# One score tile of the next attention step placed ahead of the first token product, at the ends of the second and third step

## The chip, the cores and the metric

One core of one Trainium2 chip runs the whole program. The metric is the device time of one execution in microseconds (us). Traces are of one execution each.

## The reference, cut to what matters

```python
def _attn_ref(q, k, v):                      # q, k, v: (8, 12, 448, 64)
    scores = scale * np.matmul(q, k.transpose(0, 1, 3, 2))
    attn = np.maximum(scores, 0.0) ** 2 / S
    return np.matmul(attn, v)

def _moe_ref(x, w_tok1, w_tok2, w_ch1, w_ch2):   # x: attention as (8, 448, 768)
    xt = x.transpose(0, 2, 1)
    h = np.maximum(xt @ w_tok1, 0.0) @ w_tok2    # token mixing
    u = x + h.transpose(0, 2, 1)
    h2 = np.maximum(u @ w_ch1, 0.0) @ w_ch2      # channel mixing
    return u + h2
```

## The kernel before

Attention runs in 24 steps of four heads, numbered from 0; (i,c) is score tile c (0 to 6) of step i. The program order is set by hand, and each engine works through its own list in that order. One tile is four TensorE matmuls into one of two score buffers in PSUM (the on-chip memory that matmuls write to), a relu (negative values set to zero) on ScalarE into SBUF (the on-chip memory for operands), and later a squaring on VectorE:

```python
ps_att = ctx.enter_context(tc.tile_pool(name="ps_att", bufs=2, ...))   # two score buffers
ps_acc = ctx.enter_context(tc.tile_pool(name="ps_acc", bufs=1, ...))   # acc0, acc1
ps_mm  = ctx.enter_context(tc.tile_pool(name="ps_mm", bufs=2, ...))    # "bank": shared ring of two
...
def scores(i, c, alone=False):
    ps = ps_att.tile([128, 2, 512], FP32, tag="att", name="sc_ps")
    ...                                   # 4 matmuls from qkT[i]
        nc.scalar.activation(at, ps[:, :, :S], AF.Relu)
    squares.append(at)

def square(keep=0):
    while len(squares) > keep:
        at = squares.pop(0)
        nc.vector.tensor_tensor(out=at, in0=at, in1=at, op=ALU.mult)
```

`values` multiplies squared tiles by v into acc0 and acc1; `values_out` evicts them; `x_back` transposes the result (through acc0 here) and has it copied to SBUF as x; `token1` is the first token product from x, with a relu on ScalarE; `token2` is the second. `transposes(i)` makes the transposed queries and keys of step i in the two `ps_mm` banks, and VectorE copies them out to `qkT[i]`. Steps 0 to 2 and the start of step 3 are this code (cut):

```python
for i in range(DB):                       # DB = 3
    for c in range(QC):                   # QC = 7
        scores(i, c, alone=(i, c) == (0, 2))
        ...
        square(keep=1)
        if c < 3 and i > 0:
            values(i - 1, ((2, 3), (4, 5), (6,))[c])
            if c == 2:
                values_out(i - 1, split=True)
        if c in (1, 2) and i > 1:
            token2(i - 2, early=True, rs=(c - 1,))
        ...
        if c == 4 and i > 0:
            x_back(i - 1, place="acc0", copy=nc.scalar.copy if i > 1 else None)
        if (i, c) in ((1, 3), (2, 5)):
            transposes(i + 1, "bank")
        if c == 6:
            values(i, (0, 1))
            if i > 0:
                token1(i - 1)
...
i = DB
values(i - 1, (2, 3, 4, 5))
square()
values(i - 1, (6,))
values_out(i - 1, split=True)
scores(i, 0)
token2(i - 2, early=True, between=lambda: x_back(DB - 1, place="acc0"))
scores(i, 1)
token1(i - 1)
square(keep=1)
scores(i, 2)
first = channel1_begin()
```

## Time and profile before

The median is 376.17 us in four runs (375.63 to 376.41); the profiled span is 374.7 us. The first part of the page gives, for each engine, busy time, its share of the span, and the number of instructions:

```profile
PE 365.0 (97%) x4377; PEld 201.2 (54%) x4377; DVE 212.1 (57%) x414; ACT 211.0 (56%) x313; POOL 99.1 (26%) x185
```

PE is TensorE's matmuls, PEld its weight loads, which overlap them; DVE is VectorE, ACT ScalarE. An average over the span says little on a change at 20 and 28 us, so the argument rests on rows in order of time, which the prediction shows.

### The profile page before, as it was taken

The numbers are of one execution on the slowest core, as the hardware profiler recorded it, in microseconds if no ns is written. First come the engines' busy times: TensorE is split into PE (matmuls) and PEld (weight loads), VectorE is DVE, ScalarE is ACT, GpSimd is POOL, SyncE is SP. The second block draws the span as 40 slices with busy tenths as digits, with TensorE's granted clock in tenths as the row PEclk, the third lists the DMA queues.
The fourth block names the chain that finished last, engine by engine and source line by source line (L and its number), as shares of the span: only waits on it lengthen the run. The fifth ranks groups of instructions, "written<-read, shape, count | busy, mean of one in ns | idle before, by whom it ended". The sixth has DMA issues, their size and how long they took to land.

```text
span 374.7 us, 10236 instructions
## 1 busy us (share of the span) xinstructions
PE 365.0 (97%) x4377; PEld 201.2 (54%) x4377; DVE 212.1 (57%) x414; ACT 211.0 (56%) x313; POOL 99.1 (26%) x185
## 2 busy tenths in 40 slices
PE   7889999999999999999999999999999999999996
PEld 3544555455555655565455655555555654555554
DVE  2986688756576666475554684575555755131022
ACT  3987888776345468725775457752775456311400
POOL 8956348304212403430330304412210000000000
PEclk9999999999999999999999999999999999999999
DMA  8999999923998886756765877758560534233024
GB/s 150 118 197 163 179 206 172 180 39 67 128 174 171 159 146 95 115 104 154 97 101 90 117 141 132 108 80 158 107 99 13 93 87 98 58 69 87 0 54 116
DMA packets 69566, 43.32 MB, mean 116 GB/s; under 512 B 43473, under 2 KB 66065, under 8 KB 69521
## 3 DMA queue, kind: packets, MB, share of 16 engines
q0 software_dynamic: 24496, 21.49, 40.8%
q1 hardware_dynamic: 44640, 20.75, 26.6%
q8 instruction: 34, 0.56, 0.6%
q10 hardware_dynamic: 384, 0.43, 0.4%
q14 instruction: 12, 0.09, 0.1%
HBM read 43.42 MB, written 11.01 MB: 145 GB/s over the span
## 4 chain that ended last, share of the span: by engine, by line
PE 89%; DVE 6%; ACT 1%; DMA 1%; issue 1%; POOL 0%; ACTq 0%; POOLq 0%; DVEq 0%
PE m_ps L443 29%; PE m_ps L404 28%; PE acc_ps L223 9%; PE sc_ps L190 9%; PE h_ps L353 4%; PE t_ps L312 3%; DVE at L211 2%; PE qkT_ps L140 2%; PE t_ps L294 1%; DMA q_raw<-in_q_dram 1%; DVE uT_sb L363 1%; PE t_ps L328 1%; ACT at L204 1%; DVE qkT L154 1%; PE x_ps L276 1%
## 5 line engine op out<-in xcount | busy, mean ns | idle before, releaser
L204 ACT ACTIVATE at<-sc_ps 128x896 bf16<-128x896 f32 x167 | 144.8, 924 | 49.7 <-PE sc_ps L190 49.7
L211 DVE TENSOR_TENSOR at<-at 128x896 bf16<-128x896 bf16 x168 | 97.7, 619 | 55.9 <-ACT at L204 55.9
L404 PE MATMUL m_ps<-uT_sb,wc 128*128 128x448 bf16 x564 | 115.5, 353 | 0.2 <-DVE uT_sb L363 0.2
L443 PE MATMUL m_ps<-wc,r_sb 128*128 128x384 bf16 x660 | 113.2, 326 | 0.0
L443 PEld LDWEIGHTS <-r_sb 128*128 128x128 bf16 x660 | 62.7, 98 | 46.7 <-issue 6.1
L411 ACT ACTIVATE r_sb<-m_ps 128x448 bf16<-128x448 f32 x94 | 51.3, 546 | 56.0 <-PE m_ps L404 55.6
L404 PEld LDWEIGHTS <-wc 128*128 128x128 bf16 x564 | 52.3, 98 | 53.4 <-issue 8.3
L450 DVE TENSOR_TENSOR out_sb<-m_ps,u_sb 128x384 f32<-128x384 f32 x55 | 30.5, 554 | 48.1 <-PE m_ps L443 48.1
L190 PE MATMUL sc_ps<-qkT 64*64 64x448 bf16 x672 | 53.2, 358 | 1.1 <-ACT at L204 0.9
L223 PE MATMUL acc_ps<-at,v_raw 64*64 64x448 bf16 x672 | 40.7, 351 | 1.5 <-DVE x_sb L285 0.7
L241 DVE TENSOR_SCALAR xT<-acc_ps 128x448 bf16<-128x448 f32 x45 | 26.1, 620 | 27.6 <-PE acc_ps L223 27.6
L659 POOL COPY gate<-x_sb 1x1 bf16<-1x1 bf16 x12 | 3.1, 254 | 126.9 <-DMA x_sb<-xT 126.9
L83 POOL DMA_DIRECT2D q_raw<-in_q_dram x48 | 28.9, 614 | 19.9 <-DMA wc<-in_moe_w_ch_dram 17.4
L363 DVE TENSOR_TENSOR uT_sb<-h_ps,xT 128x448 bf16<-128x448 f32 x48 | 27.7, 616 | 9.4 <-PE h_ps L353 9.3
L83 POOL DMA_DIRECT2D v_raw<-in_v_dram x48 | 29.6, 643 | 8.1 <-DMA wc<-in_moe_w_ch_dram 4.7
L338 ACT ACTIVATE r_sb<-t_ps 128x256 bf16<-128x256 f32 x36 | 11.8, 381 | 32.7 <-PE t_ps L328 28.5
L223 PEld LDWEIGHTS <-v_raw 64*64 64x64 bf16 x672 | 21.4, 106 | 15.7 <-issue 5.7
L190 PEld LDWEIGHTS <-qkT 64*64 64x64 bf16 x672 | 17.6, 105 | 21.9 <-issue 19.0
L83 POOL DMA_DIRECT2D k_raw<-in_k_dram x46 | 28.2, 634 | 1.7 <-issue 1.7
L154 DVE COPY qkT<-qkT_ps 128x896 bf16<-128x896 bf16 x44 | 25.3, 616 | 5.4 <-PE qkT_ps L140 5.4
L353 PE MATMUL h_ps<-wt,r_sb 128*128 128x448 bf16 x96 | 22.3, 353 | 0.0
L312 PE MATMUL t_ps<-x_sb,wt 128*128 128x256 bf16 x108 | 14.7, 273 | 0.0
(58 smaller groups left out, 150.7 us busy)
## 6 DMA issues: line engine op xcount, KB each, us to landing
out_dram<-out_sb SPq DMA_DIRECT2D x54, 192.0 KB, 2.9
q_raw<-in_q_dram POOLq DMA_DIRECT2D x48, 112.0 KB, 3.9
v_raw<-in_v_dram POOLq DMA_DIRECT2D x48, 112.0 KB, 4.8
k_raw<-in_k_dram POOLq DMA_DIRECT2D x46, 112.0 KB, 4.4
wc<-in_moe_w_ch_dram POOLq DMA_DIRECT2D x4, 1152.0 KB, 12.2
u_sb<-uT_sb SPq DMA_TRANSPOSE x48, 2.6
x_sb<-xT SPq DMA_TRANSPOSE x16, 3.2
k_first<-in_k_dram SPq DMA_DIRECT2D x1, 224.0 KB, 3.5
```

The costliest lines, as they stand in the source:

```text
L83: eng.dma_start(out=dst[64 * r : 64 * (r + 1)].rearrange("p g c d -> p g (c d)"), in_=src[b, h0 : h0 + 2].rearrange("g (p c) d -> p g (c d ...
L154: (nc.scalar.copy if split and r == 0 else nc.vector.tensor_copy)(sb[:, r].rearrange("n w t -> n (w t)"), parts[r][:, : 2 * S])
L190: nc.tensor.matmul(ps[64 * r : 64 * (r + 1), g, :S], lhsT=sb[h, r, 1, c * 64 : (c + 1) * 64], rhs=sb[h, r, 0, :], start=True, stop=True, s ...
L204: nc.scalar.activation(at, ps[:, :, :S], AF.Relu)
L211: nc.vector.tensor_tensor(out=at, in0=at, in1=at, op=ALU.mult)
L223: nc.tensor.matmul(ps[r][64 * g : 64 * (g + 1), :S], lhsT=v_raw[h, g, c, :], rhs=at[h, g, :], start=(c == 0), stop=(c == QC - 1), skip_gro ...
L353: nc.tensor.matmul(parts[r][:, :S], lhsT=r1[:, j, r * 128 : (r + 1) * 128], rhs=wt2[:, j, :], start=(j == 0), stop=(j == JC - 1),)
L363: nc.vector.tensor_tensor(out=uT_tiles[b // 2][:, 2 * d + r, off : off + S].rearrange("n (c p) -> n c p", c=QC), in0=parts[r][:, :S].rearr ...
L404: nc.tensor.matmul(ps[:, :S], lhsT=wc1[:, g, e * 128 : (e + 1) * 128], rhs=uT[:, g, off : off + S], start=(g == 0), stop=(g == CC - 1),)
L411: nc.scalar.activation(r2[:, e, off : off + S], ps[:, :S], AF.Relu)
L443: nc.tensor.matmul(ps[:, :HN], lhsT=r2[:, e, t * 128 : (t + 1) * 128], rhs=wc2[:, e, cols], start=(e == 0), stop=(e == EC - 1),)
L450: nc.vector.tensor_tensor(out=o[:, cols].rearrange("n (g d) -> n g d", d=128), in0=ps[:, :HN].rearrange("n (g d) -> n g d", d=128), in1=u_ ...
```

## The change

Intent: tile (2,0) at the end of the second step, and (3,0) at the end of the third, are to give ScalarE and VectorE something to do while TensorE is on the first token product.

```diff
-            scores(i, c, alone=(i, c) == (0, 2))
+            if c or i < 2:
+                scores(i, c, alone=(i, c) == (0, 2))
...
             if c == 6:
                 values(i, (0, 1))
                 if i > 0:
+                    scores(i + 1, 0)
+                    square(keep=1)
                     token1(i - 1)
...
     values_out(i - 1, split=True)
-    scores(i, 0)
     token2(i - 2, early=True, between=lambda: x_back(DB - 1, place="acc0"))
```

## The prediction

> Names used here: the program runs attention in steps of four heads; (i,c) is score tile c of step i, with i and c counted from 0, so the "second and third step" are i = 1 and 2. One score tile is four TensorE matmuls, a ScalarE relu out of PSUM, and a VectorE squaring.
>
> **What bounds the kernel now.** I read the page's chain first, then TensorE's waits from 41.9 us to the end, then the busy time by stretch.
>
> ```profile
> PE 89%; DVE 6%; ACT 1%; DMA 1%; issue 1%; POOL 0%; ACTq 0%; POOLq 0%; DVEq 0%
> ```
>
> ```profile
> PE m_ps L404 <- DVE uT_sb L363: 0.2, 1, 0.2
> PE acc_ps L223 <- DVE uT_sb L363: 0.2, 1, 0.2
> ```
>
> TensorE carries 89% of the chain that ended last. After 41.9 us it waits for other engines twice, 0.4 us together, and none of that is for a load from memory. So whatever TensorE gains or loses before 41.9 us should move the end by the same amount. The change lies in two places before that, near 20 us (end of step 1) and near 28 us (end of step 2). Next I read the time-ordered view of all engines there; columns are start, duration, engine, line, operation, count, and in brackets the idle time before it.
>
> ```profile
> 16.74 3.42 ACT L204 ACTIVATE at<-sc_ps 128x896 bf16<-128x896 f32 x4
> 19.70 0.57 PE L223 MATMUL acc_ps<-at,v_raw 64*64 64x448 bf16 x8 [0.72 <-DVE x_sb L285]
> 20.20 1.05 PE L294 MATMUL t_ps<-x_sb,wt 128*128 128x256 bf16 x8
> 21.18 0.38 PE L190 MATMUL sc_ps<-qkT 64*64 64x448 bf16 x4
> 21.29 0.60 ACT L302 ACTIVATE r_sb<-t_ps 128x512 bf16<-128x512 f32 x1 [1.12 <-PE t_ps L294]
> 21.39 0.55 PE L223 MATMUL acc_ps<-at,v_raw 64*64 64x448 bf16 x8
> 21.77 0.36 PE L190 MATMUL sc_ps<-qkT 64*64 64x448 bf16 x4
> 21.78 2.53 ACT L204 ACTIVATE at<-sc_ps 128x896 bf16<-128x896 f32 x3
> 22.72 0.62 DVE L211 TENSOR_TENSOR at<-at 128x896 bf16<-128x896 bf16 x1 [1.48 <-ACT at L204]
> 22.92 0.11 PEld L190 LDWEIGHTS <-qkT 64*64 64x64 bf16 x4 [0.37 <-issue]
> ```
>
> Here the change aims: during the first token product (20.20) ScalarE stands idle for 1.12 us and VectorE for 1.48, because no score tile is ready. TensorE itself runs without a break from 19.70 to 22.92.
>
> ```profile
> 26.19 1.08 ACT L285 COPY x_sb<-x_ps 128x1024 bf16<-128x1024 bf16 x1
> 27.00 1.15 DVE L154 COPY qkT<-qkT_ps 128x896 bf16<-128x896 bf16 x2
> 27.08 1.82 ACT L204 ACTIVATE at<-sc_ps 128x896 bf16<-128x896 f32 x2
> 27.32 0.57 PE L223 MATMUL acc_ps<-at,v_raw 64*64 64x448 bf16 x8 [0.52 <-ACT x_sb L285]
> 27.83 1.05 PE L294 MATMUL t_ps<-x_sb,wt 128*128 128x256 bf16 x8
> 28.81 1.19 PE L223 MATMUL acc_ps<-at,v_raw 64*64 64x448 bf16 x20
> 29.80 0.38 PE L190 MATMUL sc_ps<-qkT 64*64 64x448 bf16 x4
> 30.12 0.93 PE L353 MATMUL h_ps<-wt,r_sb 128*128 128x448 bf16 x4
> 31.54 0.69 DVE L285 COPY x_sb<-x_ps 128x1024 bf16<-128x1024 bf16 x1 [0.20 <-PE x_ps L276]
> 32.28 1.03 PE L294 MATMUL t_ps<-x_sb,wt 128*128 128x256 bf16 x8 [0.47 <-DVE x_sb L285]
> ```
>
> At the second place things differ. Tile (3,0) needs the transposed queries and keys of step 3, which VectorE copies out only from 27.00 to 28.15; and one of the two PSUM buffers for scores, the one of (2,5), is read by ScalarE until about 28.0 (first half of the 27.08 row). In the old order that tile ran at 29.80, when both were long done.
>
> **What the Trainium skill says.** "PSUM — Partial Sum Buffer", section "Engine vs sequencer instructions": ScalarE and VectorE queues are strict FIFO, and "MATMULs start and complete in program order". So a score tile put ahead of the token product holds that product up while it waits; nothing slips past. The trace agrees in the case at hand: during the wait of 0.72 us before 19.70 no later matmul appears. "Perfetto Trace Analysis", section "Optimization Strategy": find the gaps of the engine to be optimized, within its own regime, and make what they wait for start sooner. The gaps of 1.12 and 1.48 us are not TensorE's. Same page, section "Summary: the profiler window per engine type": the end of a TensorE instruction is estimated. I therefore count TensorE from start to start, and take an end only as a release of the next engine (the profile has 0.02 to 0.04 us between the two).
>
> **The change part by part.** No work is added or removed; each engine runs the same count of instructions. TensorE's order changes at two places, ScalarE's with it, VectorE's only at the second. Start-to-start costs, from the rows: value products of two tiles 0.38 us if 64-wide work follows (21.39 to 21.77) and 0.50 if 128-wide follows (19.70 to 20.20); a score tile 0.21 or 0.32 (29.80 to 30.12); token product 0.98 (20.20 to 21.18). ScalarE relu 0.855 (3.42 over 4) with 0.92 to its end; VectorE 0.535 each.
>
> First place. New order: values 19.70, (2,0) at 20.08, token product at 20.40, next values at 20.40 + 0.98 = 21.38 against 21.39. TensorE gains nothing. ScalarE: (2,0) is ready at 20.08 + 0.38, so its relu runs 20.48 to 21.40 instead of 21.78 to 22.70; the token relu then 21.47 (0.18 later, harmless: token2 needs it only at 22.44); relu of (2,1) at about 22.14 instead of 22.6. But (2,2) comes from TensorE at 22.92 whatever ScalarE does, and is ready at 23.30; its relu starts at 23.32, against 23.37 before (third of the 21.78 row). So of a lead of 0.4 us, 0.05 is left: ScalarE's idle time has only moved. From there to 27.3 ScalarE is full (relus, eviction, copy of x), and that is what TensorE's 0.52 us wait hangs on: value products at 27.26 instead of 27.32. VectorE runs ahead by about 0.25 us until it meets the relu of (2,4), which ends at about 26.32; then its copies of queries and keys start at 26.87 instead of 27.00 and end at 28.02.
>
> Second place. New order: values 27.26, done with at 27.64; (3,0) now waits for the buffer of (2,5) (relu 27.03 to 27.95) and for the second copy (28.02), so it finishes its start at about 28.06, a new wait of some 0.4 us. Token product about 28.3 instead of 27.83; values 28.3 + 0.98 = 29.28; token2 follows them directly: 29.28 + 0.99 + 0.12 (switch to 128-wide) = 30.39 against 30.12. That is 0.27 late. The removed score tile (0.32) repaid only part of 0.47 + 0.12. Next: eviction of the last values at 29.28 + 1.19 + 0.03 = 30.50 to 31.12, back transposes when token2 is through, 30.39 + 0.77 = 31.16; copy of x on VectorE at 31.81 to 32.50; token product at 32.54 against 32.28. The 0.47 us wait for that copy stays, since the back transposes move by as much. From here all is in the old order, TensorE full: the end moves by +0.26. With a full 0.32 between (3,0) and the token product it would be +0.33. I take +0.3.
>
> Sum: 0.0 at the first place, -0.05 carried to 27.26, +0.35 at the second: 376.11 + 0.3 = 376.4.
>
> **Rivals.** (a) The intent works: the relu of (2,0) fills the 1.12 us gap, ScalarE leads by a relu (0.855), and TensorE's waits of 0.26 (25.01, for an eviction) and 0.52 us (27.32) go. For it: both waits end on ScalarE or VectorE work. Against it: the 22.92 row, where TensorE's own order ends the lead. It would make at most 376.11 - 0.8 = 375.3. (b) The new wait is worse: the copies are still at 27.00, or TensorE pays the full switch and the token relu, now behind the relu of (3,0) on ScalarE (28.74 to 29.65, then 0.6), comes at 30.2, just ahead of the 30.39 at which token2 needs it. If it were late, another 0.3: 376.7 to 376.9. (c) The second place costs nothing, because the waits on 32.28 (0.47 us) swallow the delay: that holds only if the back transposes, which start it, do not move; they do, with token2. It would make 376.1.
>
> **Range and chances.** The three runs before spread over 0.78 us (375.63 to 376.41), more than the effect. Adding the rivals gives 375.7 to 377.0. Two per cent is 7.5 us, far above the sum of TensorE's idle time at both places, so within 2% is all but certain.
>
> **What would show it.** Right: ScalarE's idle 1.12 us before the token relu split into two shorter ones, about 0.3 before (2,0) and some before (2,2); the 0.52 us wait before the values near 27.3 still there; a new TensorE wait near 27.6 to 28.1 ended by the VectorE copy L154 or by a ScalarE relu; the token product of step 2 (32.28 before) about 0.3 us later; everything after that shifted by the same. Wrong: relu of (2,2) well before 23.3; no new wait near 27.9; that token product at or before 32.28.

## The result, and the profile after

The changed kernel took 376.48 us in the median of four runs (376.23 to 377.13) against 376.17 us; ratio 1.0013, interval 0.9995 to 1.003. A second set of rounds (told below) gave 1.0012, interval 1.0000 to 1.0024.

The chain that ended last, by engine, after:

```profile
PE 90%; DVE 3%; DMA 2%; POOL 2%; ACT 1%; issue 1%; POOLq 0%; ACTq 0%; DVEq 0%
```

TensorE still sets the end. Now the first place, rows in order of time (start, duration, engine, line, operation, count; in brackets the idle time before and what ended it):

```profile
19.57 0.57 PE L223 MATMUL acc_ps<-at,v_raw 64*64 64x448 bf16 x8 [0.75 <-DVE x_sb L285]
19.94 0.39 PE L190 MATMUL sc_ps<-qkT 64*64 64x448 bf16 x4
20.26 1.05 PE L294 MATMUL t_ps<-x_sb,wt 128*128 128x256 bf16 x8
20.38 0.92 ACT L204 ACTIVATE at<-sc_ps 128x896 bf16<-128x896 f32 x1 [0.35 <-PE sc_ps L190]
21.34 0.60 ACT L302 ACTIVATE r_sb<-t_ps 128x512 bf16<-128x512 f32 x1
22.79 0.38 PE L190 MATMUL sc_ps<-qkT 64*64 64x448 bf16 x4
23.23 0.92 ACT L204 ACTIVATE at<-sc_ps 128x896 bf16<-128x896 f32 x1 [0.26 <-PE sc_ps L190]
```

This trace reaches the first row 0.13 us sooner than the one before (19.57 against 19.70), because an input landed sooner (near 6.9 us the trace before waits 0.64 us for queries of step 0, this one doesn't), so compare distances from that row. ScalarE's gap of 1.12 us is gone: the relu of (2,0) runs in it. But (2,2), the 22.79 row, comes 3.22 us after the first row, as before (22.92 - 19.70), and ScalarE now waits 0.26 us for it.

The second place:

```profile
26.78 1.15 DVE L154 COPY qkT<-qkT_ps 128x896 bf16<-128x896 bf16 x2
26.95 2.59 ACT L204 ACTIVATE at<-sc_ps 128x896 bf16<-128x896 f32 x3
27.16 0.57 PE L223 MATMUL acc_ps<-at,v_raw 64*64 64x448 bf16 x8 [0.52 <-ACT x_sb L285]
27.98 0.38 PE L190 MATMUL sc_ps<-qkT 64*64 64x448 bf16 x4 [0.25 <-ACT at L204]
28.29 1.05 PE L294 MATMUL t_ps<-x_sb,wt 128*128 128x256 bf16 x8
29.27 1.14 PE L223 MATMUL acc_ps<-at,v_raw 64*64 64x448 bf16 x20
30.34 0.93 PE L353 MATMUL h_ps<-wt,r_sb 128*128 128x448 bf16 x4
32.53 1.03 PE L294 MATMUL t_ps<-x_sb,wt 128*128 128x256 bf16 x8 [0.47 <-DVE x_sb L285]
```

The 0.52 us wait that the intent would have removed stands. A new one has come before (3,0): the bracket says 0.25 us, and counted from start to start it is more, 27.98 - 27.16 - 0.38 = 0.44 us. From the first row to the last (the token product of step 2) it was 32.28 - 19.70 = 12.58 us; it is 32.53 - 19.57 = 12.96 us, so 0.38 us is lost.

Yet both profiled spans are 374.7 us. Of the 0.38 us, 0.13 is the earlier start of this trace. The rest lies near 182 us: a row of weight loads in the trace of before,

```profile
181.97 0.55 PEld L312 LDWEIGHTS <-wt 128*128 128x128 bf16 x6 [0.48 <-DMA x_sb<-xT]
```

waits for a transpose by DMA, and none does in the trace after. From the back transposes near 44.7 us to the last group of matmuls, TensorE took 324.18 us before (44.67 to 368.85) and 323.95 us after (44.92 to 368.87). In the traces of the experiments this stretch takes 323.96 us where it meets no such wait, and 324.00 to 324.60 us where it meets one to three. Such waits come and go between executions, so one span cannot decide a question of 0.3 us.

### The profile page after: what moved, and what is told of

Its sections match the earlier page's. It is cut to its first block, busy times and chain, and to the rows that moved or that the text cites. A ratio compares the mean times of both kernels' runs of the same rounds, so it can differ in the third digit from the quotient of the medians.

```text
span 374.7 us, 10236 instructions
## 1 busy us (share of the span) xinstructions
PE 365.7 (98%) x4377; PEld 202.0 (54%) x4377; DVE 212.5 (57%) x414; ACT 211.4 (56%) x313; POOL 99.0 (26%) x185
## 4 chain that ended last, share of the span: by engine, by line
PE 90%; DVE 3%; DMA 2%; POOL 2%; ACT 1%; issue 1%; POOLq 0%; ACTq 0%; DVEq 0%
PE m_ps L443 29%; PE m_ps L404 28%; PE acc_ps L223 9%; PE sc_ps L190 9%; PE h_ps L353 4%; PE t_ps L312 3%; PE qkT_ps L140 3%; DMA q_raw<-in_q_dram 1%; PE t_ps L294 1%; PE t_ps L328 1%; DMA k_raw<-in_k_dram 1%; ACT at L204 1%; DVE uT_sb L363 1%; POOL q_raw L83 1%; DVE at L211 1%
## 5 line engine op out<-in xcount | busy, mean ns | idle before, releaser
L338 ACT ACTIVATE r_sb<-t_ps 128x256 bf16<-128x256 f32 x36 | 11.9, 381 | 32.4 <-PE t_ps L328 28.3
```

## The experiments

For each kernel the table has the start of three TensorE groups, counted from the start of the value products near 19.7 us: the value products and the token product at the second place, and the token product of step 2. Ratios are against the kernel before of the same rounds.

| kernel | values | token product | token product of step 2 | median us | ratio (interval) |
|---|---|---|---|---|---|
| before | 7.62 | 8.13 | 12.58 | 376.17 | |
| changed | 7.59 | 8.72 | 12.96 | 376.48 | 1.0013 (0.9995 to 1.003) |
| changed again | 7.58 | 8.72 | 12.96 | 376.68 | 1.0012 (1.0000 to 1.0024) |
| first place alone | 7.59 | 8.09 | 12.54 | 376.04 | 0.9996 (0.9983 to 1.0008) |
| second place alone | 7.63 | 8.82 | 13.06 | 376.73 | 1.0016 (1.0004 to 1.0029) |
| copies early | 7.58 | 8.72 | 12.96 | 376.57 | 1.001 (0.9995 to 1.0024) |
| (3,0) behind | 7.59 | 8.09 | 13.23 | 376.94 | 0.9998 (0.9976 to 1.0019) |
| (3,0) behind, squaring held | 7.59 | 8.10 | 12.52 | 376.06 | 1.0002 (0.999 to 1.0013) |
| (2,2) supplied | 7.33 | 7.93 | 12.31 | 375.86 | 0.9986 (0.9958 to 1.0014) |

The runs of "(3,0) behind", "(2,2) supplied" and the first of "tiles in the gaps" shared rounds in which the kernel before had two of eleven runs at a mean clock of 0.994 and 0.995, 378.59 and 378.16 us; the other nine were at 0.998 or more, 375.92 to 376.86 us, mean 376.56. These two widen those intervals and lower those ratios.

**The first place alone.** Edit against the changed kernel: the move only where i == 1, and `scores(i, 0)` put back in the start of step 3.

> Only the first place is changed (tile (2,0) ahead of the first token product), the second is as before. My theory: ScalarE's lead is lost again at tile (2,2), which TensorE delivers when it did before, so the value products near 27.3 us start 0.05 us earlier against the start of the value products near 19.7 us, and the end moves by -0.05 us, ratio 1.000. Rival (the intent works): the two TensorE waits of 0.26 and 0.52 us go, up to -0.8 us, ratio 0.998.

12.54 against 12.58: 0.04 us gained, as expected. The 0.52 us wait is there, and the 0.26 us wait for an eviction is gone without effect: the next tile (2,5) waits for ScalarE's relu of (2,3) instead:

```profile
25.05 0.38 PE L190 MATMUL sc_ps<-qkT 64*64 64x448 bf16 x4 [0.17 <-ACT at L204]
```

The intent brought next to nothing here.

**The second place alone.** Edit: the move only where i == 2.

> Only the second place is changed (tile (3,0) ahead of the token product of step 1), the first is as before. My theory: tile (3,0) waits for its PSUM buffer and for the second copy of queries and keys, now ending at 28.15 us, so it pays slightly more than in the full change: token product of step 2 about 0.4 us later against the value products near 19.7 us, end +0.4 us, ratio 1.001. Rival (the waits after it swallow the delay): end unchanged, ratio 1.000.

0.48 us later, 0.08 more than expected, and slower by 0.6 us in time, by the medians of these rounds (376.73 against 376.12 us) and by the ratio. All of the change's loss is here. With the changed kernel's first place in front, ScalarE and VectorE come a little earlier and 0.10 us of it is spared.

**The copies earlier.** Edit against the changed kernel: `((1, 3), (2, 5))` becomes `((1, 3), (2, 4))` for the transposes.

> The changed kernel with the transposes of step 3 one score tile earlier, so that the copies of queries and keys are done near 27.5 us. If the wait of (3,0) is held by its PSUM buffer as well (the relu of (2,5) ends near 27.95), it starts no earlier: 8.3 to 8.4 us after the value products near 19.7 (8.41 in the changed kernel), ratio 1.001. If the copies alone hold it, it starts at 8.0 and the end is 0.35 us earlier, ratio 1.000.

VectorE's copies of queries and keys are through at 27.32 us (26.17 + 1.15), well ahead. The tile starts when it did, 8.41 us after the first row in both kernels:

```profile
28.05 0.38 PE L190 MATMUL sc_ps<-qkT 64*64 64x448 bf16 x4 [0.25 <-ACT at L204]
```

So taking away one of the two waits gives nothing: the score buffer, freed by ScalarE's relu of (2,5), holds the tile by itself. In "second place alone" the bracket names the copies. The two waits end almost together: taken singly, that relu and the second copy both end at 27.92 us in the changed kernel, and at 28.17 and 28.22 in "second place alone".

**Tile (3,0) behind the token product.** Edit against the changed kernel:

```diff
-                if i > 0:
+                if i == 1:
                     scores(i + 1, 0)
                     square(keep=1)
+                if i > 0:
                     token1(i - 1)
+                if i == 2:
+                    scores(i + 1, 0)
+                    square(keep=1)
```

> The changed kernel, but at the second place tile (3,0) stands directly behind the token product instead of ahead of it (still ahead of the last value products of step 2, so still earlier than before). By then (28.8 us) its buffer and its copies are ready. My theory: the new wait is gone and so is the loss; the end is that of the kernel before, -0.05 to 0 us, ratio 1.000. Rival (any move of that tile ahead of the value products costs, by the eviction they start): +0.2 to +0.3 us, ratio 1.001.

A miss. The wait ahead of the token product is gone (8.09), but the token product of step 2 is at 13.23, later than in the changed kernel. The ratio of 0.9998 hides this: without the two slow-clock runs of the kernel before, the means are 376.94 and 376.56 us, 0.4 us slower. Rows in order of time:

```profile
30.46 0.62 DVE L211 TENSOR_TENSOR at<-at 128x896 bf16<-128x896 bf16 x1 [0.79 <-ACT at L204]
31.01 0.62 DVE L241 TENSOR_SCALAR xT<-acc_ps 128x448 bf16<-128x448 f32 x1
31.68 0.62 PE L276 MATMUL x_ps<-ident,xT 128*128 128x128 bf16 x8 [0.57 <-DVE xT L241]
```

The squaring of (3,0) stands ahead of the eviction in VectorE's list, and its input came late, since the relu of (3,0) now lies behind the token relu. The eviction, ready since the value products, queues behind it, and the back transposes wait for that.

**The same with that squaring held back.** Edit: besides, `square()` becomes `square(keep=1)` between the last value products of step 2.

> Tile (3,0) directly behind the token product, as in the first try of that place, but its squaring is now left behind the last evictions of step 2 on VectorE instead of ahead of them. If the 0.57 us wait of the back transposes in the first try came from that squaring in VectorE's queue, it goes, and the token product of step 2 starts 12.5 to 12.6 us after the value products near 19.7 (12.58 before, 12.96 in the changed kernel, 13.23 in the first try): end -0.05 to 0 us against before, ratio 1.000. Rival (the place itself costs): still 12.9 or later, ratio 1.001 to 1.002.

12.52: the loss is gone. The tile may stand elsewhere at this place without cost if it meets its buffer free, and if its follow-up on VectorE doesn't block an eviction.

**The transposes late, in both kernels.** Edit: `((1, 3), (2, 5))` becomes `((1, 3), (2, 6))`, first in the changed kernel, then in the kernel before.

> The changed kernel with the transposes of step 3 issued one score tile later, so that their copies come on VectorE after the squaring of (2,5), near 28.5 to 29.6 us: the suspected wait of (3,0) is made about 1.6 us longer. My theory: everything behind it moves with it, 1.6 us more than the changed kernel, some 378.1 us, ratio 1.005. Rival (delays there are swallowed by later waits): within 0.3 us of the changed kernel, ratio 1.001 to 1.002.

> The control of the late transposes: the kernel before with the same transposes issued one tile later. There (3,0) runs at 29.80 us, when the late copies (28.6 to 29.8) are just done: my theory gives 0 to 0.1 us, ratio 1.000. If the late transposes cost time by themselves, this is 1.6 us longer too, ratio 1.004.

The control missed. It took 377.68 us, ratio 1.0043 (1.0028 to 1.0059). What waited there was the token product:

```profile
29.31 1.03 PE L294 MATMUL t_ps<-x_sb,wt 128*128 128x256 bf16 x8 [1.44 <-DVE qkT L154]
```

It doesn't read the transposed queries and keys; but its PSUM tile comes from the same ring of two banks as the transposes, and I had overlooked that. So this pair does not isolate the tile's wait. It does show that a delay here reaches the end: from the token product of step 0 to that of step 2 it was 12.08 us (20.20 to 32.28) and became 13.52 us (20.17 to 33.69), 1.44 us more, for 1.5 to 1.6 us in time.

The changed kernel with late transposes took 379.93 us, 1.0089 (1.0068 to 1.011), more than the 378.1 expected. Its tile (3,0) waits for the copies:

```profile
28.97 0.38 PE L190 MATMUL sc_ps<-qkT 64*64 64x448 bf16 x2 [1.44 <-DVE qkT L154]
```

Its token product of step 1 starts 10.45 us after the first row, 1.73 later than in the changed kernel; that of step 2 at 16.29 us, 3.33 later. Busy time by stretch (after the time: length, then busy time of PE, PEld, DVE, ACT and POOL with instruction counts, then the clock granted to TensorE, DMA share and GB/s):

```profile
29.90:31.00 1.10, 1.10 (x12) 0.75 (x15) 0.21 (x2) 1.03 (x2) 1.10 (x3) 0.96 1.26 200
31.00:34.00 3.00, 3.00 (x24) 1.17 (x17) 1.42 (x3) 1.03 (x2) 2.83 (x5) 0.50 1.25 198
```

For 3 us the clock was half. That is about the other 1.5 us (what set it off is not shown; see the last section). One of this kernel's four runs had a mean clock of 0.999 and took 378.19 us, close to what was expected; the other three had 0.995 and 379.92 to 380.24.

**Tile (2,2) supplied sooner.** Edit against "first place alone": (2,2) is issued directly behind (2,1), with the squaring kept in its old order.

```diff
+            if (i, c) == (2, 1):
+                scores(2, 2)             # and not at c == 2
-            square(keep=1)
+            square(keep=2 if (i, c) == (2, 1) else 1)
```

> Only the first place changed, and there tile (2,2) is also issued directly behind (2,1). If TensorE's late delivery of (2,2) is what ate ScalarE's lead, the relu of (2,2) now starts near 23.0 instead of 23.37 us, the value products near 27.3 start about 0.3 us earlier (against those near 19.7), and the end moves by -0.3 us, ratio 0.999. Rival (the lead is lost elsewhere, say in the evictions): no more than the first place alone, -0.05 us.

Two relus now follow each other on ScalarE, and the value products of the second place start 7.33 us after the first row instead of 7.62, the token product of step 2 0.27 us sooner than before:

```profile
21.38 0.55 PE L190 MATMUL sc_ps<-qkT 64*64 64x448 bf16 x8
21.79 1.73 ACT L204 ACTIVATE at<-sc_ps 128x896 bf16<-128x896 f32 x2
```

This shows that TensorE's late delivery of (2,2) ate the lead. In time the interval doesn't exclude nothing: the kernel before was spread, and one of its own six runs was at 378.68 us and a clock of 0.995. Without the runs at 0.995 and less the means are 375.96 and 376.56 us.

**Tiles in TensorE's own gaps.** Edit against "(2,2) supplied":

```diff
             if c == 6:
+                if i == 1:
+                    scores(i + 1, 0)     # ahead of the value products
                 values(i, (0, 1))
                 if i == 1:
-                    scores(i + 1, 0)
                     square(keep=1)
...
     scores(i, 1)
+    scores(i, 2)
     token1(i - 1)
-    square(keep=1)
-    scores(i, 2)
+    square(keep=2)
```

Tile (2,0) goes into TensorE's wait of 0.72 us at 19.7, and (3,2) into its wait of 0.47 us before the token product of step 2; (3,0) stays where it was before.

> Tiles placed in TensorE's own idle time, with buffers and inputs ready: (2,0) ahead of the value products near 19.7 us, in the 0.72 us wait for the copy of x; (2,2) directly behind (2,1); and (3,2) ahead of the token product of step 2, in the 0.47 us wait at 32.28. Tile (3,0) as before. My theory: -0.5 us at the first place, -0.3 us at the last, about 375.3 us, ratio 0.998. Rival (the order of tiles there does not matter): 376.1 us, ratio 1.000.

> The kernel with the tiles in TensorE's own gaps once more, because the kernel before was spread widely in its first rounds: my theory -0.8 us, about 375.3 us, ratio 0.998; if the 0.9957 of the first rounds was the chip's spread in the kernel before, the ratio now is nearer to 0.998.

The first rounds gave 375.35 us and 0.9957 (0.9937 to 0.9977), against the spread kernel before; with its two slow-clock runs left out, 375.33 over 376.56 is 0.9967. The second rounds, on another chip, gave 375.39 against 376.10 us, 0.9982 (0.9971 to 0.9994). This kernel beats both, by 0.7 us over before. The three moves were not run one by one, so the share of each is not shown. The trace of the first of them:

```profile
30.75 0.57 PE L190 MATMUL sc_ps<-qkT 64*64 64x448 bf16 x8
31.60 1.03 PE L294 MATMUL t_ps<-x_sb,wt 128*128 128x256 bf16 x8 [0.28 <-DVE x_sb L285]
32.47 1.68 PE L422 MATMUL m_ps<-uT_sb,wc 128*128 128x448 bf16 x8
```

(3,2) is the second half of the first row; the wait for x has shrunk from 0.47 to 0.28 us, and nothing stands between the token product and the channel product. From the token product of step 0 (19.98) to the channel product it is 12.49 us, before it was 13.36 (20.20 to 33.56): 0.87 us less, where 0.8 was expected; 12.50 us in the second trace.

**The changed kernel again.**

> The changed kernel itself, on the chip of the other runs of this call. My theory: +0.3 to +0.4 us, ratio 1.001; in its trace the token product of step 2 starts 12.9 to 13.0 us after the value products near 19.7 us (12.58 before). Rival (the first trace's delay was chance): 12.6.

12.96, the same as in its first trace to 0.01 us, and the ratio is the same too. The delay is no chance.

## Why the prediction was right

- The time: 376.4 was predicted, 376.48 measured, and 376.68 again. Within the range. That the number fits to 0.1 us is partly luck, since the runs of one kernel spread over 0.8 to 1.1 us and neither interval of the changed kernel is clear of 1. The sign rests on the delay in both traces and on "second place alone" (1.0004 to 1.0029).
- The first place gains 0.0, with 0.05 us carried on: measured 0.03 (7.59 against 7.62) in the changed kernel and 0.04 with that place alone. The cause named, the 22.92 row, was tested by supplying (2,2) sooner, which turned the 0.04 into 0.27 to 0.29 us. So this is shown.
- The second place: the wait for the buffer and the copies came where it was foretold. Start at "about 28.06" is 27.93 on this trace's clock (0.13 us sooner); it was 27.98. The term mis-sized is the next: "token product about 28.3" took 0.24 us from the start of (3,0), where the rows show 28.29 - 27.98 = 0.31. I had thought that the first half of the tile could start while its second waited for the second copy; but the buffer, which holds both halves, came free no sooner than that copy ended. A reading was off there too: I let the relu of (2,5) take 0.92 us and end near 28.0, where the row taken singly shows 1.01 us before (27.08 to 28.09) and 0.97 us after. This and the 0.05 us make the loss 0.38 where +0.26 to +0.33 stood.
- "From here all is in the old order, TensorE full" fits the average of the runs (0.5 us slower by the ratios, 0.3 and 0.6 us by the medians, 0.38 us lost in the trace), but the step that led to it was wrong. I took the waits of the matmul rows after 41.9 us and concluded that none was for a memory transfer. The wait of 0.48 us for the transposing DMA was there, on the weight-load row; the waits of those rows had been asked for, and the answer listed it. In the profiled span it made up for 0.23 of the 0.38 us.
- Rival (a) fell in the whole: the 0.26 us wait went, but one of 0.17 us took its place, and the 0.52 us wait stayed. What spoke against it (TensorE's order ends the lead) is what the last kernels remove. Rival (b) came in part: the step to 128-wide work took the full 0.31 us, but the token relu ended at 30.04 (29.38 + 0.66), ahead of the 30.34 at which token2 needs it, so that was not late. Rival (c) fell: the 0.47 us wait stayed in full.

What stays open: the waits on transposing DMAs after 41.9 us were seen in some traces and not in others, and no run tells why.

## What to carry to other kernels

Filling another engine's gap is worth only what it gives the engine that sets the end. Look first for the idle time of that engine, and put into it work whose inputs and buffers are ready by then; a tile that must wait for its buffer blocks all that stands behind it in the same list. When an order is changed, follow each moved piece through every list it stands in: its relu, its squaring, and the PSUM ring it shares.

## What the Trainium skill lacked or had wrong

- "TensorE: Matmul & The Clock Gate", section "What's actually happening", says the clock gate has two states, of which the lower is half of the upper; the 0.50 between 31 and 34 us in the late-transposes run agrees. Its section "HAM oscillation — how this bites in real kernels" gives as the rule no idle gaps longer than about 3.4 us. Here the clock halved though no wait of TensorE from 20 us on was longer than 1.44 us. (The same page does say that frequent short idle times bring the clock down too, but not how much of them.) What set it off is not shown. From 27.0 to 30.4 us TensorE was busy for 1.80 of 3.40 us here, and for 1.91 us in the kernel before with late transposes, which had a wait of 1.44 us too and stayed at 1.00; and one of four runs of the changed kernel with late transposes kept a mean clock of 0.999. The kernel before also had two of eleven runs at 0.994 and 0.995 in one set of rounds, and took 1.6 to 2.0 us longer in them than on average in the others.
- "TensorEngine Tiling (Array Packing)", section "Key Properties", says that changing the tiling mode drains TensorE, but gives no cost. Eight 64-wide matmuls were followed after 0.38 us by 64-wide and after 0.50 us by 128-wide ones, so 0.12 us more with a change here.
- "Perfetto Trace Analysis", section "Optimization Strategy", says to find the gaps on the engine to be optimized. It lacks that TensorE's wait can show on the weight load alone: the 0.48 us for the DMA near 182 us was on that row and on no matmul row. (In "first place alone" the same wait was 0.67 us on the weight load and 0.23 us on the matmul.)
